# Random V blocks of 18 pairs: gathered by GpSimd with row lists, in place of SP's block transfers

## The chip, the cores and the metric

The kernel runs on one core of a Trainium2 chip. The metric is the device time of one execution in microseconds, taken as the median of the runs. Engines are called PE (TensorE), DVE (VectorE), ACT (ScalarE), POOL (GpSimd) and SP (SyncE).

## The reference

Block-sparse attention, and then a two-layer network over its output:

```python
batch, n_heads, seq, head_dim = (4, 8, 768, 64)
block, n_rand = 32, 3
n_blocks = seq // block                                   # 24
rand_blocks = np.random.randint(0, n_blocks, size=(n_blocks, n_rand))

scores = scale * np.matmul(q, k.transpose(0, 1, 3, 2))
mask = np.abs(blk_i - blk_j) <= 1
mask = mask | (blk_i == 0) | (blk_j == 0) | (blk_i == n_blocks - 1) | (blk_j == n_blocks - 1)
for qb in range(n_blocks):
    for kb in sampled_blocks[qb]:
        mask[qb * block:(qb + 1) * block, kb * block:(kb + 1) * block] = True
scores = np.where(mask, scores, -1e9)
attn = softmax(scores)
x = (attn @ v), heads side by side                        # 3072 x 512
h = x @ w_in                                              # 3072 x 2048
g = h * (1.0 / (1.0 + np.exp(-beta * h)))
return (g @ w_out).astype(np.float32)                     # 3072 x 512
```

The three random key blocks of a query block are the same for all heads and all batches, and are known only at run time.

## The kernel before

**Pairs.** The 22 inner query blocks of a batch are handled two at a time: 11 pairs per batch, 44 pairs `n` in all, pair `n` being pair `p` of batch `b`. For each of its two query blocks (`g` = 0, 1) a pair needs eight key blocks: three random ones, three neighbours, and the first and the last block. Pairs 26 to 32 belong to the third batch, pairs 33 to 43 to the fourth.

**Steps of a pair.** POOL copies the random K blocks out of the transposed K (`kg`, L634); POOL or DVE copies the neighbours (`kn`, L312). PE computes the scores (`sc`, L753 for the mask, L763 for Q·K). DVE takes the maximum (`mx`, L776), ACT the exponential (`ex`, L784), DVE the reciprocal (`rc`, L801), POOL or DVE multiplies by it (`nrm`, L807). PE transposes the probabilities (`tp`, L821), DVE or ACT brings them to SBUF (`ptv`), PE multiplies with V (`av`, L848 from pair 16 on, 16 matmuls per pair), and DVE and ACT write the result into `xT`. There are three buffers for the K blocks and for the probabilities.

**V.** Each batch's V is stored to a table `VT[b]` in DRAM (L594), with the 512 numbers of all heads of one token in a row. The tile of a pair, `VG`, has four buffers from pair 8 on, so its transfers wait for `av` of pair `n - 4`. In it 96 partitions hold the three random blocks and 96 the three neighbours of each `g`; 32 more hold the first and the last block, which stay in place within a batch: three later pairs of a batch copy them on DVE (`vres`, L312 with `VG<-VG`). From pair 4 on the random blocks come by six transfers from SP, 32 rows of 1 KB each, whose addresses SP has loaded into registers for up to two pairs at a time (`vv`, L663). All transfers of `VG` are L714.

**The first and last query blocks** attend to all keys. They are handled per batch (L911 to L971); their matmuls with V (L965) wait for DVE's copies into `PTG` (L953).

**The network** runs in eight groups `G` of tokens (256 or 512 tokens): PE's h (L1027), ACT's tanh (L1033), DVE's product (L1038), PE's y (L1054). ACT scales each 128 x 512 result (`oe`, L316) and SP stores it (`od`, L1072; L1074 and L1075 where the rows are split into two stores). The last result of the run is of the split kind. Groups wait for the `xT` columns of their pairs.

**The order.** Every step is a task with an engine or a choice of engines, a duration, a priority and dependencies. `Plan.run` plays the tasks through with these durations and fixes the order of each engine's instructions and, where a task has a choice, its engine; on the chip every engine then works through its own list in order, and semaphores do the waiting. `Plan.OFFSET` shifts the priorities of single tasks.

Of the kernel before, what the change touches and what calls it, by code (L numbers as in the profile page):

```python
# [216 lines left out]
def kernel(  # L217
# [11 lines left out]
    nc = tc.nc  # L229
# [31 lines left out]
    NHOT, NV = 0, 2  # L261
    NHL, UP = 4, 1024.0
    WIDE = 16

# [33 lines left out]
    t_sb = [sb(f"t{i}", [P, 512]) for i in range(NT)]  # L298
    osb = [sb(f"osb{i}", [P, D_MODEL], FP32) for i in range(NO)]
    VT = [dram.tile([S, D_MODEL], FP16, name=f"VT{b}") for b in range(B)]  # L300
    banks = [psum.tile([P, 512], FP32, name=f"bank{i}") for i in range(8)]
# [88 lines left out]
    for part, f in enumerate((emit_mask0, emit_mask1, emit_mask2)):  # L390
# [135 lines left out]

    trK, trQ, evK, evQ, vperm, vtab = {}, {}, {}, {}, {}, {}
    later = {b: [] for b in range(B)}
    for b in range(B):
        pr = prep_prio(b)  # L530
        if b:
            vperm[b] = []
            for nm, t, raw in (("V", v, RV), ("K", k, RK), ("Q", q, RQ)):
                tr = {"K": trK, "Q": trQ}.get(nm)
                for f in range(2):
# [18 lines left out]
        for nm, s16, dstT, tr, ev in (("K", RK, KT, trK, evK), ("Q", RQ, QT, trQ, evQ)):  # L554
            for hp in range(NHP):
                def emit_tr(nm=nm, s16=s16, b=b, hp=hp):
# [22 lines left out]
        if b == 0:  # L579
            vperm[0], vtab[0] = [], []  # L580
            for f in range(2):
                cs = slice(f * HH * D, (f + 1) * HH * D)
                vperm[0].append(add(f"vperm0.{f}", "DVE", 0.95, lambda f=f, cs=cs: copy_on(
                    "DVE", Vn[0][:, :, cs].rearrange("p j (h d) -> p h j d", h=HH),
                    v_stage[:, f * HH:(f + 1) * HH, :].rearrange("p h (j d) -> p h j d", j=J)),
                    deps=[v0ld[f]], prio=-73))
                vtab[0].append(add(f"vtab0.{f}", "SP", 0.45, lambda cs=cs, vt_rows=vt_rows: nc.sync.dma_start(
                    out=vt_rows[:, :, cs], in_=Vn[0][:, :, cs]),
                    deps=[vperm[0][f]], prio=-77.5, dma=0.95, hw=1))

            for f in range(2):
                ld0["Q", f].deps += vperm[0][:QV[f]]
        else:
            vtab[b] = [add(f"vtab{b}", "SP", 0.4, lambda b=b, vt_rows=vt_rows: nc.sync.dma_start(  # L594
                out=vt_rows, in_=Vn[b % 2]), deps=vperm[b], prio=pr + 5, dma=1.9, slack=1.0, hw=1)]

# [12 lines left out]
    order_pairs = [(b, p) for b in range(B) for p in range(NPAIR)]  # L609
    xlate, picks = [], []  # L610
    held_n, vv, vv_of, vg_last = {}, None, None, None
    RND = 0.18
# [3 lines left out]
    for n, (b, p) in enumerate(order_pairs):  # L616
# [10 lines left out]

        def emit_kg(b=b, p=p, kt32=kt32, kg32=kg32):
            _, vals = nc.values_load_multi_w_load_instructions(
                offP[0:1, p, 0:6], engines=(ET.Pool,), min_val=0, max_val=(NB - 1) * W,  # L630
                skip_runtime_bounds_check_because="block numbers lie below the number of blocks")
            for g in range(2):
# [29 lines left out]
        def emit_vv(n=n, p=p):  # L662
# [3 lines left out]
                skip_runtime_bounds_check_because="block numbers lie below the number of blocks")[1]  # L666
        if n >= NSEL and (p % NV == 0 or n == NSEL):
            held_n[n] = min(NV - p % NV, NPAIR - p)
            vv = add(f"vv{n}", "SP", 0.7 + 0.03 * 6 * (held_n[n] - 1), emit_vv,
                     deps=[t_idx] + (vg[n - 4] if n >= 4 else []), prio=-45.5 if n < NSEL + 4 else pr - 1)  # L670
            vv_of = n
        elif n < NSEL:
            vv = None

        vt = VT[b]

        def moves(n=n, vgb=vgb, vt=vt, i0=i0, first=head_v, w0=6 * (n - vv_of) if n >= NSEL else 0):
            if first and n >= 2 * NVG:
# [18 lines left out]
            elif i0 + 1 < NB - 2:  # L697
                yield 0.6, lambda v: (
                    vgb[0:3 * BLK, :, 1, :],
                    bass.AP(tensor=vt.tensor, offset=vt.offset + (i0 - 1) * BLK * D_MODEL,  # L700
                            ap=[[D_MODEL, 3 * BLK], [BLK * D_MODEL, 2], [1, D_MODEL]]))
            else:
                yield 0.3, lambda v: (vgb[0:3 * BLK, 0, 1, :], vt[(i0 - 1) * BLK:(i0 + 2) * BLK, :])
                yield 0.1, lambda v: (vgb[0:BLK, 1, 1, :], vt[(NB - 1) * BLK:NB * BLK, :])
                yield 0.2, lambda v: (vgb[BLK:3 * BLK, 1, 1, :], vt[i0 * BLK:(i0 + 2) * BLK, :])
# [5 lines left out]
        for k_, (cost, f) in enumerate(moves()):  # L711
            def emit_vg(vv_of=vv_of if n >= NSEL else None, f=f):
                o, i = f(held.get(vv_of))
                nc.sync.dma_start(out=o, in_=i)  # L714
            vg[n].append(add(f"vg{n}.{k_}", "SP", 0.5, emit_vg,
                             deps=[vv] + vtab[b] + ([av[vlast(n)]] if vlast(n) >= 0 else []) +
                             ([ld["Q", 0, hp] for hp in range(NHP)] if NVG <= n < 2 * NVG else []),
                             prio=vprio(n, k_), dma=cost, hw=1))

# [95 lines left out]
        def emit_tp(n=n, pb=pb):  # L815
            o = bank16(("T", n))
            for g in range(2):
                for c in range(2):
                    for u in range(2):
# [3 lines left out]
        tp[n] = add(f"tp{n}", "PE", 0.45, emit_tp, deps=[nrm[n]] if nrm[n] else [ex[n, 0], ex[n, 1]], prio=pr - 0.5, lat=0.2,  # L823
                    opens=(("T", n),))
        ptv[n] = add(f"ptv{n}", {"DVE": 0.61, "ACT": PTA}, None, lambda eng, n=n: copy_on(
            eng, PT[n % NPT], bank16(("T", n))),
            deps=[tp[n]] + ([av[n - NPT]] if n >= NPT else []), prio=pr - 0.5, closes=(("T", n),))

        wide = n >= WIDE

        def emit_av(n=n, vgb=vgb, wide=wide, late=late, hl=HL[n % NHL]):
            o = bank(("O", n))
            pt = PT[n % NPT].rearrange("x (g c u m) -> x g c u m", g=2, c=2, u=2)

# [65 lines left out]
    for b in range(B):  # L900
        for w, (blk, u) in enumerate((bl, u) for bl in (NB - 1, 0) for u in range(2)):
# [28 lines left out]
            def emit_ge(m=m, s_=s_, pg=pg):  # L930
                for hf in range(2):
                    nc.scalar.activation(  # L932
                        out=pg[:, hf * (S // 2):(hf + 1) * (S // 2)], in_=bank(("GS", m, hf))[:, 0:S // 2],
                        func=AF.Exp, bias=s_[:, 2:3], scale=1.0, accum_out=s_[:, 3 + hf:4 + hf])
# [12 lines left out]
            def emit_gt(m=m, pg=pg):  # L947
                o = bank16(("GT", m))
                pj = pg[:, :].rearrange("x (p j) -> x j p", j=J)
                for j in range(J):  # L950
                    nc.tensor.transpose(out=o[:, j * P:(j + 1) * P], in_=pj[:, j, :], identity=identity)
            gt[m] = add(f"gt{m}", "PE", 0.34, emit_gt, deps=[gn[m]], prio=pr, lat=0.2, opens=(("GT", m),))
            gptv[m] = add(f"gptv{m}", "DVE", 0.47, lambda m=m, w=w: nc.vector.tensor_copy(  # L953
# [37 lines left out]
    for b in range(2, B):  # L991
        old = [x[n] for n, (bb, _) in enumerate(order_pairs) if bb == b - 2 for x in (kg, kn)] + gsc_all[b - 2]
        oldq = [sc[n] for n, (bb, _) in enumerate(order_pairs) if bb == b - 2] + gsc_all[b - 2]
        for hp in range(NHP):
            trK[b, hp].deps += old
            trQ[b, hp].deps += oldq
        for t in vperm[b]:
# [11 lines left out]
    for G, sz in enumerate(sizes):  # L1009
# [38 lines left out]
        for s in range(sz // 4):  # L1048
# [20 lines left out]

            def emit_od(ob=ob, base=base, row=row):  # L1070
                if row + P <= S:
                    nc.sync.dma_start(out=out[base + row:base + row + P, :], in_=ob)  # L1072
                else:
                    nc.sync.dma_start(out=out[base + row:base + S, :], in_=ob[0:S - row, :])  # L1074
                    nc.sync.dma_start(out=out[base:base + row + P - S, :], in_=ob[S - row:P, :])  # L1075
            out_dma.append(add(f"od{G}.{s}", "SP", 0.9 if row + P > S else 0.45, emit_od, deps=[te],
                               prio=at(0.5 + 2.0 * s / sz), slack=ODS, dma=0.7, hw=2 if row + P > S else 1))
            nout += 1
# [35 lines left out]
```

## Time and profile before

| | us |
|---|---|
| median of 3 runs | 307.89 (307.64 to 308.00) |
| the profiled execution | 306.66 |
| its span | 304.9 |
| PE busy | 284.7 (93%) |
| DVE busy | 241.3 (79%) |
| ACT busy | 219.8 (72%) |
| POOL busy | 172.9 (57%) |
| transfers of 32 KB into VG from SP, landing | 220, median 2.6 |

The profiled execution is one run with the profiler on; its time beside the span has 1.76 us at the start and the end that the span leaves out. An engine's busy time counts the instructions that compute; POOL's transfers count as busy while POOL prepares them, SP's do not. Matmuls overlap in the pipeline, so a busy PE is one that has work without a gap.

### The profile page before, as it was taken

To read this page: it belongs to the slowest core of one execution; us is meant where nothing else is said; L and a number is where in the kernel's file an instruction comes from. 1 tells how busy PE (TensorE), PEld (TensorE's weight loads), DVE (VectorE), ACT (ScalarE), POOL (GpSimd) and SP (SyncE) were. 2 spreads that over 40 slices of the span, in tenths; PEclk is the share of its full clock that TensorE was granted. 3 is DMA by queue.
4 is the path that set the end of the run, shared out by engine and by line. 5 is a ranking of instruction groups with operands and counts; after the bars stand their busy time and mean duration, and the time that the engine had idled before them with its cause. 6 is when DMAs were issued, how large, how long until landed. Compare 5 with 4: busy or idle time off the path is not lost.

```text
span 304.9 us, 11891 instructions
## 1 busy us (share of the span) xinstructions
PE 284.7 (93%) x4209; PEld 177.3 (58%) x4209; DVE 241.3 (79%) x562; ACT 219.8 (72%) x639; POOL 172.9 (57%) x513
## 2 busy tenths in 40 slices
PE   2699869999999899999998999999999999999994
PEld 0455658657855785665556555556555555554671
DVE  4857989999999999999999579989789765780260
ACT  3347669889788999898759599978689837771461
POOL 3079895044689678899784486868646942100000
PEclk9999979999999999999999999999999999999999
DMA  7999999978999462479943633234343242101202
GB/s 254 370 295 207 233 208 231 221 219 136 165 208 183 119 190 74 123 145 166 210 124 116 203 123 97 73 85 124 100 155 106 75 121 90 37 0 57 83 1 69
DMA packets 43445, 44.17 MB, mean 145 GB/s; under 512 B 6005, under 2 KB 39414, under 8 KB 43386
## 3 DMA queue, kind: packets, MB, share of 16 engines
q1 hardware_dynamic: 31056, 32.13, 35.1%
q0 software_dynamic: 12320, 11.27, 24.8%
q8 instruction: 33, 0.54, 0.7%
q14 instruction: 26, 0.21, 0.2%
q10 hardware_dynamic: 10, 0.01, 0.0%
HBM read 45.23 MB, written 9.44 MB: 179 GB/s over the span
## 4 chain that ended last, share of the span: by engine, by line
PE 70%; DVE 18%; DMA 6%; issue 2%; ACT 2%; SPq 1%; POOL 0%; DVEq 0%
PE bank L1027 26%; PE bank L1054 20%; PE bank L821 5%; DMA VG<-VT 4%; DVE ST L776 4%; PE bank L848 4%; PE bank L560 3%; PE bank L729 3%; DVE SG L925 3%; DVE VG L312 3%; DMA g<-in_k_dram 3%; PE bank L753 2%; PE bank L763 2%; PE bank L856 2%; DVE PTG L953 2%
## 5 line engine op out<-in xcount | busy, mean ns | idle before, releaser
L784 ACT ACTIVATE PP<-bank,ST 128x256 f16<-128x256 f32 x176 | 81.4, 479 | 20.6 <-DVE ST L776 12.4
L1027 PE MATMUL bank<-xT,w_in_sb 128*128 128x256 f16 (+1 forms) x512 | 94.0, 328 | 1.4 <-DVE g L1038 0.9
L1054 PE MATMUL bank<-w_out_sb,g 128*128 128x512 f16 x384 | 92.3, 380 | 0.0
L1038 DVE SCALAR_TENSOR_TENSOR g<-t,bank 128x512 f16<-128x512 f16 (+1 forms) x128 | 66.5, 546 | 19.4 <-ACT t L1033 19.0
L1033 ACT ACTIVATE t<-bank,beta_sb 128x512 f16<-128x512 f32 (+1 forms) x128 | 70.4, 594 | 13.5 <-PE bank L1027 9.6
L807 POOL TENSOR_SCALAR PP<-PP,ST 128x256 f16<-128x256 f16 x132 | 63.4, 497 | 27.6 <-DVE ST L801 27.6
L634 POOL COPY KG<-KT 128x64 f32 x264 | 52.0, 247 | 32.4 <-PE bank L763 18.8
L1027 PEld LDWEIGHTS <-w_in_sb 128*128 128x128 f16 x512 | 53.7, 115 | 25.8 <-issue 4.6
L776 DVE TENSOR_REDUCE ST<-bank 128x2 f32<-128x512 f32 x88 | 57.4, 680 | 3.4 <-PE bank L763 2.1
L1054 PEld LDWEIGHTS <-g 128*128 128x128 f16 x384 | 34.4, 98 | 38.2 <-issue 4.9
L784 ACT ACTIVATION_READ_ACCUMULATOR PP<-bank,ST 128x1 f32 x176 | 37.0, 210 | 0.0
L316 ACT ACTIVATE osb<-bank 128x512 f32<-128x512 f32 x24 | 14.5, 605 | 19.6 <-PE bank L1054 19.5
L312 DVE COPY PT<-bank 128x1024 f16<-128x1024 f16 x39 | 26.7, 685 | 2.4 <-PE bank L821 1.6
L821 PE MATMUL bank<-identity,PP 128*128 128x128 f16 x352 | 28.0, 224 | 0.3 <-ACT PP L784 0.3
L943 POOL TENSOR_SCALAR PG<-PG,SG 128x768 f16<-128x768 f16 x16 | 14.4, 900 | 23.9 <-ACT PG L932 19.8
L821 PEld LDWEIGHTS <-PP 128*128 128x128 f16 x352 | 22.8, 100 | 7.6 <-issue 1.3
L312 DVE CAST xT<-bank 64x256 f16<-64x256 f32 (+1 forms) x33 | 13.9, 420 | 8.4 <-ACT xT L310 7.4
L848 PEld LDWEIGHTS <-VG 128*128 128x128 f16 x448 | 16.5, 98 | 6.7 <-DMA VG<-VT 1.0
L932 ACT ACTIVATE PG<-bank,SG 128x384 f16<-128x384 f32 x32 | 18.3, 585 | 2.4 <-DVE SG L927 2.2
L312 POOL COPY KG<-KT 128x384 f32<-128x384 f32 (+3 forms) x47 | 19.6, 438 | 0.4 <-PE bank L763 0.4
L763 PE MATMUL bank<-KG,QT 64*32 64x256 f16 x704 | 18.0, 269 | 1.1 <-issue 1.1
L848 PE MATMUL bank<-PT,VG 128*128 128x64 f16 x448 | 17.7, 193 | 0.1
(107 smaller groups left out, 309.8 us busy)
## 6 DMA issues: line engine op xcount, KB each, us to landing
VG<-VT SPq DMA_DIRECT2D x220, 32.0 KB, 2.6
VG<-VT SPq DMA_DIRECT2D x32, 192.0 KB, 2.6
out_dram<-osb SPq DMA_DIRECT2D x20, 256.0 KB, 2.4
RV<-in_v_dram POOLq DMA_DIRECT2D x6, 384.0 KB, 6.4
RK<-in_k_dram POOLq DMA_DIRECT2D x6, 384.0 KB, 8.3
VT<-Vn SPq DMA_DIRECT2D x3, 768.0 KB, 3.9
RQ<-in_q_dram POOLq DMA_DIRECT2D x6, 384.0 KB, 6.4
w_in_sb<-in_moe_w_in_dram POOLq DMA_DIRECT2D x8, 256.0 KB, 8.0
```

The costliest lines, as they stand in the source:

```text
L312: (nc.vector if eng == "DVE" else nc.gpsimd).tensor_copy(out=out, in_=in_)
L634: nc.gpsimd.tensor_copy(out=kg32[:, g, :, (SR + r) * W:(SR + r + 1) * W], in_=kt32[:, :, bass.ds(vals[3 * g + r], W)])
L763: nc.tensor.matmul(bk[u][hp * BLK:(hp + 1) * BLK, g * 256:(g + 1) * 256], lhsT=QT[b % 2][u * D:(u + 1) * D, hp, (i0 + g) * BLK:(i0 + g + 1 ...
L776: mx[n, u] = add(f"mx{n}.{u}", "DVE", 0.6, lambda n=n, u=u, sb_=sb_: nc.vector.tensor_reduce(out=sb_[:, 0, 2 * u:2 * u + 2], in_=bank(("S" ...
L784: nc.scalar.activation(out=pb[:, u, g, :], in_=bank(("S", n, u))[:, g * 256:(g + 1) * 256], func=AF.Exp, bias=sb_[:, 0, 2 * u + g:2 * u + ...
L807: (nc.vector if eng == "DVE" else nc.gpsimd).tensor_scalar(out=pb[:, u, g, :], in0=pb[:, u, g, :], scalar1=sb_[:, 2, 2 * u + g:2 * u + g + ...
L821: nc.tensor.transpose(out=o[:, s * P:(s + 1) * P], in_=pb[:, u, g, c * P:(c + 1) * P], identity=identity)
L848: nc.tensor.matmul(o[:, (g * NHP + hp) * 2 * BLK:(g * NHP + hp + 1) * 2 * BLK], lhsT=vgb[:, g, c, hp * P:(hp + 1) * P], rhs=pt[:, g, c, :, ...
L1027: nc.tensor.matmul(o[:, 0:TW], lhsT=w_in_v[:, c, f // 4, f % 4, :], rhs=xT[:, c, c0:c0 + TW], start=(c == 0), stop=(c == NHP - 1))
L1033: lambda G=G, f=f, TW=TW, tt=tt: nc.scalar.activation(out=tt[:, 0:TW], in_=bank(("H", G, f))[:, 0:TW], func=AF.Tanh, bias=0.0, scale=beta_ ...
L1038: lambda G=G, f=f, TW=TW, tt=tt, gg=gg: nc.vector.scalar_tensor_tensor(out=gg[:, f, 0:TW], in0=tt[:, 0:TW], scalar=1.0, in1=bank(("H", G, ...
L1054: nc.tensor.matmul(o[:, :], lhsT=gg[:, f, s * P:(s + 1) * P], rhs=w_out_sb[:, f, :], start=(f == 0), stop=(f == N_FFC - 1))
```

## The change

From pair 26 on (`IG`), the random V blocks are fetched by POOL's indirect transfers. Each takes a list of 96 row numbers, one per partition, and fetches the 96 rows of `VT[b]`; there are two per pair, one for each `g`. The lists are columns of a tile `rows96`, made once near the start: POOL writes a few constants (`rowc`), PE adds 32 x block number and the row within the block by four matmuls of one row (`rows`), DVE copies them as integers (`rowlist`). SP's register loads end with pair 25. The plan books POOL with 0.9 us for each of these transfers; they wait for the list, the table and `av` of pair `n - 4`. The neighbours and the edge blocks stay with SP.

Three further edits are active. The eight transposes of a pair come in the order `u, g, c`, and the matmuls with V read accordingly. The exponential of the first and last query blocks is written in the order in which it is transposed, so that ACT reads PSUM with a stride and PE's transposes read contiguously. The last result of the run is scaled in halves by ACT and DVE, and its two stores are issued by SP and ACT. The plan's duration for the tables of V is 0.45 in place of 0.40.

The diff also brings paths that its constants turn off (`TD`, `GD`, `KD`, `NBP`, `ODP`, and `TBE = "SP"`): transposes by DMA and plain transfers from POOL. They are left out here. Its core:

```diff
+    IG, IGT = 26, 0.9
+    NI = NB - 2
+    rows96 = sb("rows96", [3 * BLK, NI], I32)
+    cE = sb("cE", [1, 4, 3 * BLK])
+    sf16 = sb("sf16", [1, 3, NI])
+    mi96 = sb("mi96", [1, 3, BLK], I32)
+
+    def emit_rc():
+        V = nc.gpsimd
+        V.iota(mi96, pattern=[[0, 3], [1, BLK]], base=0, channel_multiplier=0, allow_small_or_imprecise_dtypes=True)
+        V.memset(cE[:, 0:3, :], 0.0)
+        for r_ in range(3):
+            V.memset(cE[:, r_, r_ * BLK:(r_ + 1) * BLK], float(BLK))
+        V.tensor_copy(out=cE[:, 3, :], in_=mi96[:, :, :].rearrange("o r m -> o (r m)"))
+        V.tensor_copy(out=sf16, in_=sf[:, :, :].rearrange("o a r -> o r a"))
+    t_rc = add("rowc", "POOL", 1.0, emit_rc, deps=[t_idx], prio=60)
+
+    def emit_rows():
+        o_ = bank("rows")[0:3 * BLK, 0:NI]
+        for r_ in range(3):
+            nc.tensor.matmul(o_, lhsT=cE[0:1, r_, :], rhs=sf16[0:1, r_, :], start=(r_ == 0), stop=False)
+        nc.tensor.matmul(o_, lhsT=cE[0:1, 3, :], rhs=ones[0:1, 0:NI], start=False, stop=True)
+    t_rows = add("rows", "PE", 0.2, emit_rows, deps=[t_rc, t_ident], prio=80, lat=0.2, opens=("rows",))
+    t_list = add("rowlist", "DVE", 0.1, lambda: nc.vector.tensor_copy(
+        out=rows96, in_=bank("rows")[0:3 * BLK, 0:NI]), deps=[t_rows], prio=80, closes=("rows",))
...
-        if n >= NSEL and (p % NV == 0 or n == NSEL):
-            held_n[n] = min(NV - p % NV, NPAIR - p)
+        if NSEL <= n < max(IG, 2 * NVG) and (p % NV == 0 or n == NSEL):
+            held_n[n] = min(NV - p % NV, NPAIR - p, max(IG, 2 * NVG) - n)
...
-            for g in range(2 if n >= NSEL else 0):
+            for g in range(2 if n >= max(IG, 2 * NVG) else 0):
+                yield 0.5, (lambda v, g=g, p=p: (vgb[0:3 * BLK, g, 0, :], vt[:, :], rows96[:, 2 * p + g:2 * p + g + 1])), 3
+            for g in range(2 if NSEL <= n < max(IG, 2 * NVG) else 0):
                 for r in range(3):
...
+            eng = "POOL" if (n >= max(NBP, 2 * NVG) and where) or where == 3 else "SP"
...
+                if where == 3:
+                    o, i, rows_ = f(None)
+                    nc.gpsimd.indirect_dma_start(
+                        out=o, out_offset=None, in_=i, in_offset=bass.IndirectOffsetOnAxis(ap=rows_, axis=0))
+                    return
...
+            vg[n].append(add(f"vg{n}.{k_}", eng, 0.5 if eng == "SP" else IGT if where == 3 else 0.65, emit_vg,
+                             deps=([vv] if eng == "SP" and vv else [kg[n]] if where == 2 else [t_list] if where == 3 else []) + vtab[b] + ([av[vlast(n)]] if vlast(n) >= 0 else []) +
                              ([ld["Q", 0, hp] for hp in range(NHP)] if NVG <= n < 2 * NVG else []),
-                             prio=vprio(n, k_), dma=cost, hw=1))
+                             prio=vprio(n, k_), dma=cost, hw=int(eng == "SP")))
...
-                        s = (g * 2 + c) * 2 + u
+                        s = (u * 2 + g) * 2 + c
...
                     nc.scalar.activation(
-                        out=pg[:, hf * (S // 2):(hf + 1) * (S // 2)], in_=bank(("GS", m, hf))[:, 0:S // 2],
+                        out=pg[:, :].rearrange("x (j p) -> x j p", j=J)[:, :, hf * hw_:(hf + 1) * hw_],
+                        in_=bank(("GS", m, hf))[:, 0:S // 2].rearrange("x (p j) -> x j p", j=J),
                         func=AF.Exp, bias=s_[:, 2:3], scale=1.0, accum_out=s_[:, 3 + hf:4 + hf])
...
+            if G == len(sizes) - 1 and s == sz // 4 - 1 and row + P > S:
+                te.emit, te.on = lambda ob=ob, G=G, s=s: scale_on(
+                    "ACT", ob[:, 0:256], bank(("Y", G, s))[:, 0:256], 0.5), {"ACT": 0.35}
+                tf = add(f"of{G}.{s}", "DVE", 0.35, lambda ob=ob, G=G, s=s: scale_on(
+                    "DVE", ob[:, 256:512], bank(("Y", G, s))[:, 256:512], 0.5), deps=list(te.deps), prio=te.prio,
+                    closes=(("Y", G, s),))
+                for q, en, r0, r1, d0 in ((nc.sync, "SP", 0, S - row, base + row), (nc.scalar, "ACT", S - row, P, base)):
+                    out_dma.append(add(f"od{G}.{s}{en}", en, 0.45, lambda q=q, ob=ob, r0=r0, r1=r1, d0=d0: q.dma_start(
+                        out=out[d0:d0 + r1 - r0, :], in_=ob[r0:r1, :]), deps=[te, tf], prio=te.prio, dma=0.4, hw=1))
```

More of the change, by code (lines that the diff above doesn't have):

```diff
@@ L262 @@
     NHL, UP = 4, 1024.0
+    by_dma = lambda n: n >= TD[0] and n % TD[1] < TD[2]
+    TD = (99, 1, 1)
+    GD = 9
+    KD = 9
+    IG, IGT = 26, 0.9
+    TBE = "SP"
+    tq = lambda: nc.sync if TBE == "SP" else nc.gpsimd
+    tbk = dict(dma=1.9, hw=1) if TBE == "SP" else dict(dma=1.9)
+    NBP, ODP, RP = 99, (), 0
     WIDE = 16
@@ L299 @@
     osb = [sb(f"osb{i}", [P, D_MODEL], FP32) for i in range(NO)]
+    KQ = [dram.tile([NHP, S, P], FP16, name=f"KQ{i}") for i in range(2)]
     VT = [dram.tile([S, D_MODEL], FP16, name=f"VT{b}") for b in range(B)]
@@ L610 @@
     xlate, picks = [], []
+    held_k = {}
     held_n, vv, vv_of, vg_last = {}, None, None, None
```

125 lines of the change are left out of this document (91 added, 34 removed).

## The prediction

> **What bounds the kernel now.** I read the page first, then the windows view by stage, then the waits of TensorE (PE), the timelines of GpSimd (POOL) and SyncE (SP), and the end of the run.
>
> ```profile
> span 304.9 us, 11891 instructions
> PE 284.7 (93%) x4209; PEld 177.3 (58%) x4209; DVE 241.3 (79%) x562; ACT 219.8 (72%) x639; POOL 172.9 (57%) x513
> ...
> PE   2699869999999899999998999999999999999994
> ...
> POOL 3079895044689678899784486868646942100000
> ```
>
> PE's row is 9 almost throughout from the twelfth slice; POOL's row has room in the second half. The windows (columns: start:end, length, then busy time and count of PE, PEld, DVE, ACT, POOL) say where:
>
> ```profile
> 120.00:150.00 30.00, 29.81 (x427) 17.15 (x425) 29.41 (x69) 26.35 (x84) 27.41 (x75) 1.00 0.78 154
> 150.00:165.00 15.00, 14.18 (x242) 8.73 (x242) 14.47 (x32) 9.64 (x32) 9.86 (x27) 1.00 0.52 124
> ...
> 210.00:225.00 15.00, 14.51 (x223) 9.02 (x222) 12.41 (x25) 10.12 (x29) 9.90 (x28) 1.00 0.40 117
> ...
> 155.00:247.00 92.00, 90.69 (x1320) 53.26 (x1319) 78.08 (x158) 70.97 (x214) 63.02 (x192) 1.00 0.39 115
> ```
>
> From 150 to the last matmul at 300.9 PE stands still for 0.82 + 0.49 = 1.3 us, and the waits view of that stretch names the whole of it:
>
> ```profile
> PE bank L965 <- DVE PTG L953: 1.3, 3, 0.8
> ```
>
> No matmul there waits for V: the transfers that the change touches are hidden already. The rest of PE's idle time (some 15 us) lies before 150, and 4.0 us behind the last matmul.
>
> The change acts from the gathers of pair 26, which wait for the P·V matmuls of pair 22. L848 has 16 matmuls per pair, from pair 16 on; the windows by that line have 22 pairs left at 150, so pair 22 is the first of them, at 154.3. The last gather, for pair 43, waits for pair 39, at 246.2. So all of it falls in 155 to 247, the last row above.
>
> **Part by part: SP.** Taken off: 18 pairs x 6 = 108 transfers of 32 KB and ten register loads.
>
> ```profile
> 178.37 28.08 SPq L714 DMA_DIRECT2D VG<-VT  x45
> ...
> L663 SPq TENSOR_LOAD <-offV x22: 722/752/1995, 18.7 to 233.3; - x22
> ```
>
> 45 issues in 28.08 us are 0.62 us each; 108 x 0.62 + 10 x 0.75 = 75 us of SP's queue. On the path it is worth 0: pair n's blocks are asked for once pair n-4 is done, some 20 us (four pairs at 92/18 = 5.1 us) ahead, and they land 1.9 us after issue. What comes earlier is the output stores behind them, for which PE does not wait in this stretch (view above). If that cover were gone the landing time, 1.9 us, would show per pair.
>
> **POOL.** Added: 36 gathers of 96 rows. No view has one; the nearest rows are the plain transfers that POOL issues:
>
> ```profile
> L543 POOL DMA_DIRECT2D RQ<-in_q_dram x6 | 4.7, 789 | 0.0
> ...
> L519 POOL DMA_DIRECT2D w_out_sb<-in_moe_w_out_dram x8 | 4.1, 522 | 0.4 <-POOL w_out_sb L499 0.3
> ```
>
> Lower end 0.52 (64 partitions). Upper end 0.79 plus 0.75, the register load from memory above, as the price of reading the list: 1.54. I take 0.8: a gather has 96 pieces, fewer than RQ's 128 x 4, and reads a list on top. (The plan in the changed code books 0.9, which is no measurement.) Then 36 x 0.8 = 28.8, and POOL has 63.0 + 28.8 = 91.8 us of work in 92 us. It cannot be that full; the plan can give the copies of neighbouring K blocks to VectorE (DVE): those that POOL runs there sum to 9.0 us in its timeline. POOL and DVE together then hold 63.0 + 78.1 + 28.8 = 169.9 of 184 us, 92%. The row 120 to 150 held 27.41 + 29.41 = 56.8 of 60, 95%, with six transfers of POOL among them, and PE lost 0.19 us in 30. So I cost it at 0 on the path. The cover is gone where the two fill more than that row: 0.947 x 184 = 174.3, less 141.1, over 36 gives 0.92 us per gather. Above that PE, whose order is fixed, waits 36 us for each us of excess.
>
> A gather holds back what POOL has behind it, the K copies of the next pair (score matmuls wait for these) and the normalisation (1.84 us; the transposes wait for it), if its own waits come late: pair n-4, the table of V and the list. POOL stands still for 92 - 63 = 29 us there, mostly for DVE's reciprocals, so a gather of 0.8 fits such gaps in part. Its transfer meets no bulk load: in 155 to 247 no load of POOL is issued. Landing: 6.4 us is the median of RQ and RV, 1.9 that of the blocks now; both under 20.
>
> At one place POOL is slowed by DVE. First DVE's timeline, then POOL's, with start and duration in front:
>
> ```profile
> 155.66 0.93 DVE L312 COPY VG<-VG 32x2048 f16<-32x2048 f16 x1
> ```
>
> ```profile
> 154.69 2.69 POOL L807 TENSOR_SCALAR PP<-PP,ST 128x256 f16<-128x256 f16 x4
> ...
> 167.35 1.84 POOL L807 TENSOR_SCALAR PP<-PP,ST 128x256 f16<-128x256 f16 x4 [1.70 <-DVE ST L801]
> ```
>
> Four normalisations take 1.84 as a rule and 2.69 beside that copy: 0.85 lost of 0.93. Three such copies (pairs 34 to 36, after 209) fall among the gathers: at most 3 x 0.93 = 2.8 us more, 0.08 per gather, so 0.88, still under 0.92 but near. The Trainium skill, "SBUF — State Buffer", section "SBUF: two separate sides", says that a DMA issued from GpSimd cannot have its descriptors written while DVE holds the port pair that they share, and that SP's are immune; section "A bandwidth-pool intuition that's wrong" has one growing from about 620 to 3100 ns. By that, an estimate from the page, three gathers cost 2.5 us more each, a gather 1.0 on average and the sum 3 us more. The trace agrees for POOL's arithmetic (0.85 of 0.93 above) and shows no gather.
>
> The lists themselves: seven small operations on POOL at 0.13 to 0.24 each, about 1.4 us, behind `idx` at 3.5; POOL then stands idle for 11.7 us to 15.28. Four one-row matmuls (0.3 each by the start-to-start of L430) fall before PE's first transpose at 10.39, and one 0.2 us copy on DVE, which is idle for 0.8 before 9.77. Cost 0; 0.2 if the copy lands between the first casts.
>
> **The other edits.** The order of the pair's eight transposes and the strided read of the global rows' exponentials keep the counts. L316's evictions read PSUM strided already, 768 elements in 0.81 us against 512 contiguous ones in 0.60, no dearer per element: 0. Last output: now
>
> ```profile
> 300.89 0.60 ACT L316 ACTIVATE osb<-bank 128x512 f32<-128x512 f32 x1 [2.86 <-PE bank L1054]
> 301.51 0.33 SPq L1074 DMA_DIRECT2D out_dram<-osb  x1
> 301.89 0.42 SPq L1075 DMA_DIRECT2D out_dram<-osb  x1
> ```
>
> Halves on ScalarE (ACT) and DVE: 0.39 each (L316's 128x256 form has a median of 0.393) instead of 0.60, 0.2 saved. Both stores at once: the second, which lands 2.0 after 301.89, no longer comes last, but the first (2.3 after 301.51) does: 0.1 more. Sum 0.3; ends 0.2 and 0.6 (were both issue steps gained).
>
> **Sum.** The edits move the plan's order in the pairs, and the 1.3 us of PE's waits for PTG are redrawn; between 0 and all of it I take half, 0.6. On the profiled execution: 306.66 (span 304.9 and 1.76 around it) - 0.3 - 0.6 = 305.8. The median of the runs is 1.23 above that execution, so 307.0.
>
> **Rivals.** *POOL becomes the bound.* For it: 0.88 against 0.92, and 63 us of other work. Against: fewer pieces than any plain transfer's. Decides from 0.92 us per gather; at 1.03, 36 x 0.11 = 4.0, less 0.3: 311.6; at 1.1, 6.5 - 0.3: 314.1. Chance 0.15. *Gathers stretched by DVE's copies*, a place of its own: if all six copies of V's edge rows after 154 meet a gather, 6 x 0.93 / 36 = 0.16, so 0.96 each and 36 x 0.04 = 1.4, less 0.3: 309.0. The stretched normalisation speaks for it, that three of the six lie at the very start against it. Chance 0.06. (The page of the Trainium skill named above is the rule behind this one.) *The work given to DVE delays the pairs* (maximum, reciprocal and copies of transposes are on DVE, 96% busy in 150 to 165): 18 pairs with 0.1 us of wait each, 1.8 - 0.3: 309.4. Chance 0.12. *Only the end is saved*, since PE was full: 307.6, chance 0.12. That SP's queue bounded something unseen is against the waits view; it adds to the low end alone.
>
> **How the numbers follow.** The forecast has 0.55; about 0.6 us (0.2%) is what a measurement of this kernel can tell from none, and with more than 0.3 of the 1.3 regained it shows: 0.46 faster, 0.09 same. The last rival gives 0.11 same and 0.01 faster, the other three 0.33 slower. Faster 0.47, same 0.20, slower 0.33. The forecast's own range is 306.0 (0.6 and 1.3 regained) to 307.7 (0.2 and none). The whole reaches from 305.6 (0.4 more before 150, where PE has idle time and the plan books the tables of V at 0.45 and not 0.40, which may move the order) to 311.5, a gather of about 1.03.
>
> **What would show it.** Right: gathers of 0.7 to 0.9 us on POOL, PE idle below 1.3 us from 150 to its last matmul, neighbour K copies moved to DVE, SP's VG issues down by 108, the last store at about 301.3. Wrong: gathers over 0.92 us, POOL at 95% from 155 to 247, and PE's transposes waiting for POOL's PP; or PE waiting for DVE's ST in that stretch.

## The result and the profile after

The changed kernel took 325.35 us as the median (324.11 to 325.81), the kernel before 307.76 beside it: a ratio of 1.0577 (95% interval 1.0528 to 1.0625), 17.6 us slower, where 307.0 was predicted and 311.5 was the upper end. Three later comparisons of the same changed kernel gave 1.0255, 1.0213 and 1.0542; the two sizes are a finding of their own, taken up below.

The page after, the lines that answer to the first fence of the prediction:

```profile
span 324.0 us, 11614 instructions
PE 293.5 (91%) x4213; PEld 181.4 (56%) x4213; DVE 250.7 (77%) x578; ACT 218.6 (67%) x637; POOL 205.8 (64%) x544
...
PE   2699889999998999999989899698879989999994
...
POOL 4158992045788769999698598799978896200000
```

POOL has 32.9 us more of work, PE's row has 6, 7 and 8 in the second half where it had 8 and 9. The windows (columns as before) put it in the predicted stretch:

```profile
120.00:150.00 30.00, 29.87 (x437) 17.36 (x436) 29.44 (x73) 26.47 (x86) 27.89 (x81) 1.00 0.68 134
150.00:165.00 15.00, 14.16 (x192) 8.00 (x190) 14.60 (x30) 9.77 (x32) 11.78 (x24) 1.00 0.68 145
210.00:225.00 15.00, 13.84 (x193) 7.32 (x191) 14.45 (x33) 9.15 (x34) 13.75 (x33) 1.00 0.25 77
155.00:247.00 92.00, 81.70 (x1131) 46.35 (x1130) 72.97 (x148) 59.38 (x178) 77.46 (x174) 1.00 0.35 105
```

PE loses 10.3 us in 155 to 247 (before: 1.3), and with fewer matmuls done there it ends later. SP's part came as counted: 164 issues of `VG` from SP (272 before) and 12 register loads (22 before), the last at 152.0:

```profile
L802 SPq DMA_DIRECT2D VG<-VT x164: 304/316/1293, 15.9 to 265.8; - x164
...
L736 SPq TENSOR_LOAD <-offV x12: 725/752/1966, 18.8 to 152.0; - x12
```

The gather had no row before. First its group on the page, then three of them in POOL's timeline:

```profile
L798 POOL DMA_INDIRECT VG<-VT,rows x36 | 34.7, 965 | 8.2 <-issue 5.3
```

```profile
177.24 0.94 POOL L798 DMA_INDIRECT VG<-VT,rows  x1 [0.30 <-PE bank L943]
178.48 0.92 POOL L798 DMA_INDIRECT VG<-VT,rows  x1 [0.30 <-issue]
179.71 0.92 POOL L798 DMA_INDIRECT VG<-VT,rows  x1 [0.30 <-issue]
```

The reader should add two columns here. A gather is busy for 0.965 us on average, and POOL stands still for 8.2 us just before the 36: 0.16 ahead of a gather that follows arithmetic, 0.30 ahead of one that follows a gather (the releasers named there are long done, or "issue"). POOL is held for (34.7 + 8.2) / 36 = 1.19 us per gather; from one start to the next it is 1.23. The waits of PE from 155 on, where the old kernel had one line of 1.3 us, begin:

```profile
PE bank L1162 <- DVE xT L327: 2.8, 1, 2.8
PE bank L943 <- DVE PT L327: 1.7, 2, 0.9
PE bank L943 <- DVE ST L889: 1.2, 1, 1.2
PE bank L909 <- POOL PP L895: 1.1, 4, 0.5
PE bank L943 <- issue: 1.0, 1, 1.0
```

Few name POOL. The longest ends at a DVE cast (`xT`), and that cast stood behind copies of DVE that ran beside POOL's work. DVE's timeline, then POOL's:

```profile
203.54 2.88 DVE L327 COPY KG<-KT 128x256 f16<-128x256 f16 x3
206.46 0.43 DVE L327 CAST xT<-bank 64x256 f16<-64x256 f32 x1
```

```profile
203.56 1.12 POOL L707 COPY KG<-KT 128x64 f32 x6
204.67 2.01 POOL L895 TENSOR_SCALAR PP<-PP,ST 128x256 f16<-128x256 f16 x4
```

POOL goes without a gap from the gather at 202.62 to 206.7, and three neighbour copies of DVE take 2.88 us beside it; PE's y waits for the cast that follows them. In experiment 5 the same three took 1.35 us and POOL's copies 1.31 in place of 1.12. So the two seem to hold each other up, and which of them is held changes from run to run. Late landing is not the price: one weight load of PE waits for `VG` from 155 on (1.2 us, at 238.0), in experiment 11 none does.

### The profile page after: what moved, and what is told of

Same layout as the page of the kernel before. It is cut to its first block, busy times and chain, and to the rows that moved or that the text cites. A ratio compares the mean times of both kernels' runs of the same rounds, so it can differ in the third digit from the quotient of the medians.

```text
span 324.0 us, 11614 instructions
## 1 busy us (share of the span) xinstructions
PE 293.5 (91%) x4213; PEld 181.4 (56%) x4213; DVE 250.7 (77%) x578; ACT 218.6 (67%) x637; POOL 205.8 (64%) x544
## 4 chain that ended last, share of the span: by engine, by line
PE 51%; DVE 20%; DMA 8%; issue 7%; POOL 6%; ACT 5%; POOLq 2%; SPq 1%; DVEq 0%; ACTq 0%
PE bank L1162 17%; PE bank L1135 15%; PE bank L817 4%; DVE g L1146 4%; DMA VG<-VT 4%; PE bank L909 4%; DVE ST L864 3%; DVE SG L1020 3%; PE bank L943 3%; PE bank L629 3%; POOL KG L707 3%; DMA g<-in_k_dram 2%; DVE PT L327 2%; ACT PP L872 2%; DMA w_out_sb<-in_moe_w_out_dram 2%
## 5 line engine op out<-in xcount | busy, mean ns | idle before, releaser
L1135 PE MATMUL bank<-xT,w_in_sb 128*128 128x256 f16 (+1 forms) x512 | 95.4, 332 | 1.8 <-DVE g L1146 1.0
L707 POOL COPY KG<-KT 128x64 f32 x264 | 51.9, 245 | 20.4 <-DVE KT L327 10.6
L864 DVE TENSOR_REDUCE ST<-bank 128x2 f32<-128x512 f32 x88 | 57.6, 680 | 7.7 <-PE bank L1162 2.9
L1162 PEld LDWEIGHTS <-g 128*128 128x128 f16 x384 | 34.7, 98 | 41.6 <-issue 7.7
L798 POOL DMA_INDIRECT VG<-VT,rows x36 | 34.7, 965 | 8.2 <-issue 5.3
L327 DVE COPY PT<-bank 128x1024 f16<-128x1024 f16 x40 | 27.4, 684 | 6.7 <-PE bank L909 4.8
L909 PE MATMUL bank<-identity,PP 128*128 128x128 f16 x352 | 29.9, 228 | 2.1 <-POOL PP L895 1.1
L331 ACT ACTIVATE osb<-bank 128x512 f32<-128x512 f32 (+1 forms) x24 | 14.3, 596 | 21.9 <-PE bank L1162 21.0
L851 PE MATMUL bank<-KG,QT 64*32 64x256 f16 x704 | 19.4, 279 | 2.3 <-POOL KG L707 1.2
```

Source lines behind the costliest of these rows:

```text
L327: (nc.vector if eng == "DVE" else nc.gpsimd).tensor_copy(out=out, in_=in_)
L798: nc.gpsimd.indirect_dma_start(out=o, out_offset=None, in_=i, in_offset=bass.IndirectOffsetOnAxis(ap=rows_, axis=0))
L864: mx[n, u] = add(f"mx{n}.{u}", "DVE", 0.6, lambda n=n, u=u, sb_=sb_: nc.vector.tensor_reduce(out=sb_[:, 0, 2 * u:2 * u + 2], in_=bank(("S" ...
L909: nc.tensor.transpose(out=o[:, s * P:(s + 1) * P], in_=pb[:, u, g, c * P:(c + 1) * P], identity=identity)
L1135: nc.tensor.matmul(o[:, 0:TW], lhsT=w_in_v[:, c, f // 4, f % 4, :], rhs=xT[:, c, c0:c0 + TW], start=(c == 0), stop=(c == NHP - 1))
L1162: nc.tensor.matmul(o[:, :], lhsT=gg[:, f, s * P:(s + 1) * P], rhs=w_out_sb[:, f, :], start=(f == 0), stop=(f == N_FFC - 1))
```

## Experiments

Each comparison has its own runs of the kernel before (medians 307.4 to 308.0 us). The first four experiments shared a chip (A), the next eight another (B), the four after them chip A again, the last two a third (C); the chip of the first comparison was not recorded.

**1. All edits but the gathers.** `-    IG, IGT = 26, 0.9`, `+    IG, IGT = 99, 0.9`: no pair is gathered; the lists, the order of the transposes, the strided read, the split end stay.

> The changed kernel with IG = 99: the random V blocks of all pairs come from SP as before, the other edits stay (row lists, order of the transposes, strided exponential, split end, 0.45 booked for the tables). Theory A (a gather holds POOL for 1.23 us, 0.94 and a gap of 0.30, where the plan books 0.90): 307.4, 0.3 below the kernel before for the split end. Theory B (the redrawn order itself is poor, whatever a gather takes): 307.4 as well. Theory C (the 3 us that the changed kernel is behind at 150, before its first gather, come from the other edits): 310 to 311.

308.23 against 307.95 us, 1.0012 (0.9988 to 1.0037). The other edits neither cost nor gain what can be measured; the loss belongs to the gathers and what the plan makes of them.

**2. The gathers booked at 1.25 us.** `+    IG, IGT = 26, 1.25`: the plan knows about the true price.

> The changed kernel with 1.25 us booked for a gather in place of 0.90. Theory A: PE's order then fits what POOL does, so of the 17.6 us some 5 to 10 come back: 315 to 320. Theory B: another order, no rule for its sign: 320 to 330. Theory C: 325.

317.67 us, 1.0317 (1.0281 to 1.0354). A plan with the right duration does not find room for the work, though it loses less than the plan that books 0.9: the changed kernel took 325.3 us on the same chip (experiment 15).

**3. and 4. The changed order with a plain transfer, and with none.** In the changed order each gather is a plain POOL transfer of 96 fixed rows (experiment 3), or is left out (4); the blocks that `VG` holds are then not the selected ones.

```diff
-                    nc.gpsimd.indirect_dma_start(
-                        out=o, out_offset=None, in_=i, in_offset=bass.IndirectOffsetOnAxis(ap=rows_, axis=0))
+                    nc.gpsimd.dma_start(out=o, in_=i[0:3 * BLK, :])     # 3; in 4 nothing
```

> The changed kernel with its order unchanged; each gather is replaced by a plain transfer from POOL of the same 96 x 1 KB into the same place, from the first 96 rows of the table, so the random blocks of V from pair 26 on are not the drawn ones. Theory A: 0.5 to 0.6 us and a gap of 0.3 or less, at or under the 0.90 booked: 308 to 311. Theory B: as the changed kernel, 322 to 326. Theory C: 3 us over the kernel before, 311, if A holds otherwise.

> The changed kernel with its order unchanged; the gathers are left out, so from pair 26 on the random blocks of V are what the buffer held. Theory A: POOL is early everywhere, 307 to 309. Theory B: 322 to 326. Theory C: 310 to 311.

309.70 us, 1.0071 (1.0040 to 1.0102), and 310.48 us, 1.0072 (1.0047 to 1.0097). The plain transfer's group:

```profile
L798 POOL DMA_DIRECT2D VG<-VT x36 | 19.6, 547 | 2.1 <-PE bank L942 2.1
```

So the redrawn order by itself costs some 2 us. Without gathers PE waits 2.2 us from 155 on, all of it for DVE (1.3 before). Another 0.55 us of POOL per fetch is free. PE's waits show 0.9 of the 2 us; where the rest lies was not looked for. All that the changed kernel loses beyond this comes with the gather.

**5. The changed kernel again.** No edit.

> The changed kernel itself, beside the others on one chip, for its clock in the slices from 30 to 60 us (0.72 in its profile, 0.94 in the kernel before). If the lower clock belongs to the program: 324 to 326 and 0.7 again. If it was that chip's or that run's: about 322 and 0.9, and the 3 us by which its gathers began late are gone; the loss behind 150 stays 14 to 16 either way.

315.14 against 307.36 us, 1.0255 (1.0223 to 1.0287): the gathers are as long as before (965 ns), the loss is 10 us smaller. No reading of the expectation had that.

**6. A third of the rows.** `+ (vgb[0:BLK, g, 0, :], vt[:, :], rows96[0:BLK, 2 * p + g:2 * p + g + 1])`: each gather fetches 32 rows, two of three random blocks are left out.

> The changed kernel, order unchanged, with each gather cut to 32 of its 96 rows; the other 64 rows of the random blocks of V keep what the buffer held. If a gather's time on POOL is mostly a fixed part (reading the list, starting): 0.8 to 0.95 us and 320 or more. If it goes with the rows: 0.4 to 0.6 us and 308 to 312, as with plain transfers.

312.88 us, 1.0192 (1.0159 to 1.0226). The groups of POOL:

```profile
L798 POOL DMA_INDIRECT VG<-VT,rows x36 | 32.6, 905 | 8.3 <-issue 5.0 <-PE bank L1135 1.4 <-PE bank L943 0.9
```

64 rows fewer save 0.06 us of 0.965: the time is nearly all fixed, and shorter lists buy little, 5.5 us lost in place of 7.8. The duration came as expected for a fixed price, the total of 320 did not.

**7. Gathers from pair 35 on only.** `+    IG, IGT = 35, 1.25`: 18 gathers, where POOL has more room.

> The changed kernel with gathers from pair 35 only, 18 in place of 36, and 1.25 us booked. If the loss that stays with 1.25 booked from pair 26 on (9.7 us) is POOL's capacity, half the gathers in the half where POOL has more room cost little: 308 to 311. If each gather costs the same wherever it stands: 9.7 / 2 = 4.9, so 312.8. Other orders can add about 2 of either sign.

308.20 us, 1.0039 (1.0017 to 1.0060). Half the gathers cost 0.84 us, not half of the loss of experiment 5. Place and booking changed along with the number, but the reading is that of experiment 10 too: a gather has no price of its own on the path; what counts is whether POOL is full.

**8. SP freed and nothing added.** The kernel before, with its 108 random transfers from pair 26 on left out (those rows of `VG` are old).

```diff
+                if n >= 26 and cost == RND:
+                    return
```

> The kernel before, order unchanged, with SP's 108 transfers of random V blocks from pair 26 on left out (these blocks are what the buffer held). If SP's queue is off the path, as predicted: 307.9. If it held something back: 306 or less, and this would be the most that any change of who issues them can bring.

307.82 us, 1.0017 (0.9996 to 1.0039). In this order even a fetch that costs no engine anything would have gained nothing that can be measured.

**9. Two plain transfers per gather.** 48 fixed rows each, not the selected ones.

```diff
+                    nc.gpsimd.dma_start(out=o[0:48, :], in_=i[0:48, :])
+                    nc.gpsimd.dma_start(out=o[48:96, :], in_=i[48:96, :])
```

> The changed kernel in its order, each gather replaced by two plain GpSimd transfers of 48 fixed rows each (the same bytes into VG, not the selected blocks): 72 plain transfers in place of 36 gathers. One plain transfer of 96 rows took 0.547 us; if two of half the rows take 0.5 to 0.55 each, GpSimd is held 1.0 to 1.1 us per gather, as much as by the gather with its gap (0.94 to 0.97 and 0.16 to 0.30). Theory A (GpSimd's time counts, whatever takes it): as the changed kernel on the same chip within 2 us, 2 to 3% above before. Theory B (something of the gather itself costs, its gaps or its hold on DVE's copies): near the plain transfer's 1.007, at most 1.012.

311.13 against 307.65 us, 1.0125 (1.0095 to 1.0156): between the two theories. The pair holds POOL for 0.526 + 0.508 = 1.03 us, and no gap lies before either (groups of POOL):

```profile
L798 POOL DMA_DIRECT2D VG<-VT x36 | 18.9, 526 | 0.0
L799 POOL DMA_DIRECT2D VG<-VT x36 | 18.3, 508 | 0.0
```

**10. One gather per pair.** `+ if where == 3 and k_ % 2 == par: return`: the gather of `g` = 1 is left out.

> The changed kernel in its order, with the gather of g=1 of each pair left out (those rows of VG keep old values): 18 gathers. Theory A (GpSimd has room for about 0.8 us per gather, so for nearly one gather of 0.95 plus its gap per pair): 1.007 to 1.011, like the order without any gathers. If every gather costs a share of its own, whatever room there is: half way between 1.007 and the changed kernel of the same chip (about 1.016 or more).

309.71 us, 1.0055 (1.0035 to 1.0075): no dearer than the order without any gather (1.0072 on chip A).

**11. The changed kernel a third time.** No edit.

> The changed kernel unchanged, a third time. It gave 1.0577 in the first comparison and 1.0255 in the second. If the spread is a matter of the chip and of when PE's clock falls early: between the two, with every gather at 0.92 to 0.98 us again, and windows of 155 to 247 us with GpSimd at 13 to 14 of 15 us busy. If the first comparison was out of the ordinary: 1.02 to 1.03.

314.42 us, 1.0213 (1.0188 to 1.0238).

**12. The split end alone.** The kernel before with the last output's edit and nothing else.

> The kernel before with the last output alone split (half of its copy on DVE, half on ACT, its two stores on two queues); nothing else of the change. The prediction's term: 0.2 to 0.6 us less, ratio 0.998 to 0.9993. The rival reading after the run without gathers (1.0012): nothing measurable, within 0.2% of 1.

307.44 us, 0.9997 (0.9979 to 1.0015). The timeline at the end of this run:

```profile
300.39 0.38 ACT L316 ACTIVATE osb<-bank 128x256 f32<-128x256 f32 x1 [2.86 <-PE bank L1054]
300.80 0.42 DVE L318 TENSOR_SCALAR osb<-bank 128x256 f32<-128x256 f32 x1 [5.53 <-ACT osb L316]
301.25 0.33 SPq L1078 DMA_DIRECT2D out_dram<-osb  x1
301.26 0.38 ACTq L1078 DMA_DIRECT2D out_dram<-osb  x1
```

DVE begins its half when ACT's has ended: from the start of the scaling to the first store it is 0.86 us, against 0.62 with one piece. DVE waits for ACT's `osb`, so the halves are not side by side, and what the second store gains is spent. The plan set no such order between them; what put the wait there was not looked into.

**13. and 14. The gather's hold without a gather, and more than it.** Experiment 9 with a memset that nobody reads, and with three plain transfers of 32 rows.

```diff
+                    nc.gpsimd.memset(mi96[:, :, :].bitcast(FP16), 0.0)     # 13, behind the two of 9
+                    for r_ in range(3):                                    # 14, in their place
+                        nc.gpsimd.dma_start(out=o[r_ * BLK:(r_ + 1) * BLK, :], in_=i[r_ * BLK:(r_ + 1) * BLK, :])
```

> The changed kernel in its order, each gather replaced by two plain GpSimd transfers of 48 fixed rows (0.99 us together where they follow each other) and one memset of 192 elements that nobody reads (estimated 0.2 to 0.25 us from the 288 elements in 0.328 and the 128 in 0.195), so that GpSimd is held 1.19 to 1.24 us, as by the gather with its gap (1.23 start to start where two follow). The blocks fetched aren't the selected ones. Theory A (the hold alone): as the changed kernel of the same chip within 0.4%, 1.019 to 1.026. Theory B (a gather costs more than its hold): near the two plain transfers' 1.0125, at most 1.016.

> The changed kernel in its order, each gather replaced by three plain GpSimd transfers of 32 fixed rows, about 1.48 us of GpSimd per gather (0.50 for one where they follow). Not the selected blocks. Theory A, with GpSimd the bound beyond about 0.9 us per gather: 36 gathers longer by 0.49 us than two plain transfers make 17.6 us, most of it on the path: 1.04 to 1.07. If GpSimd's hold is mostly covered: 1.02 to 1.03.

316.83 against 307.78 us, 1.0282 (1.0218 to 1.0346); the memset took 0.264, so POOL was held 1.30 us per gather, 0.11 more than by the gather. The changed kernel took 325.3 on this chip (experiment 15), so here the hold alone, theory A, does not make the whole loss. Three transfers are (55.2 + 1.9 of gaps) / 36 = 1.59 us: 326.73, 1.0614 (1.0536 to 1.0691). The window of 13 shows POOL full:

```profile
155.00:247.00 92.00, 87.25 (x1216) 49.79 (x1214) 78.90 (x160) 66.43 (x198) 91.72 (x254) 1.00 0.35 107
```

With the plain transfers alone (experiments 4, 3, 9, 13, 14; only 9 ran on chip B) the loss against the time that POOL is held is: 2.5 us at 0, 1.8 at 0.55, 3.5 at 1.03, 9.1 at 1.30, 19.0 at 1.59: flat, then 0.57 us of loss per us held (over 36 fetches), then 1.0. Read off at the gather's 1.19 it gives 3.5 + 0.57 x 36 x 0.16 = 6.8 us. Experiment 11 lost 6.8, experiment 5 7.8; at the 1.136 of experiment 6 it gives 5.6, and 5.5 was measured. On chip B the hold explains the loss to within 1 us: a gather costs what any other work of that length on POOL costs.

**15. and 16. The changed kernel a fourth time, and the booking of 1.25 again**, on the chip of experiments 1 to 4.

> The changed kernel unchanged, a fourth time, for its spread and as the yardstick of this chip. 1.02 to 1.03 with no place where all engines stand still at once, or 1.05 to 1.06 with such places (0.44 and 0.90 us in the first profile, and the later order of the engines out of step).

> The gathers booked at 1.25 us, a second time. It gave 1.0317, with one standstill of all engines of 0.33 us after four gathers in a row. If booking the true price helps: at or below the changed kernel of this chip. If the standstill made its loss: 1.02 without it. If the longer booked order is itself worse: 1.03 again.

325.32 us, 1.0542 (1.0481 to 1.0604), as in the first comparison; 318.21 us, 1.0327 (1.0268 to 1.0387). Experiment 16 is 7 us below 15, as its first reading asked, but it has standstills as well, so it does not tell the three readings apart. In the slices between 30 and 60 us PE's clock was 0.94 in this run (0.72 in the first), so the early clock is not the cause of the 10 us. From 155 to 247 it was 0.96 here and 1.00 in the first, with the same loss. The timelines of PE, DVE and POOL in experiment 15:

```profile
178.91 0.28 PE L851 MATMUL bank<-KG,QT 64*32 64x256 f16 x5
180.01 0.45 PE L851 MATMUL bank<-KG,QT 64*32 64x256 f16 x11 [0.82 <-issue]
```

```profile
176.70 0.43 DVE L327 CAST xT<-bank 64x256 f16<-64x256 f32 x1 [2.34 <-ACT xT L325]
180.10 1.29 DVE L864 TENSOR_REDUCE ST<-bank 128x2 f32<-128x512 f32 x2 [2.97 <-PE bank L1162]
```

```profile
178.06 0.92 POOL L798 DMA_INDIRECT VG<-VT,rows  x1 [0.30 <-issue]
178.99 0.58 POOL L707 COPY KG<-KT 128x64 f32 x3
180.23 0.59 POOL L707 COPY KG<-KT 128x64 f32 x3 [0.66 <-PE bank L1162]
```

PE stops after five of sixteen matmuls of one group, POOL after three of six copies, DVE before a maximum whose scores PE had ended at 176.2; all three go on within 0.25 us. From 179.57 to 180.01, and again for 0.89 us from 237.86, no engine computes. The first profile has the same two places (0.44 and 0.90 us), each at the end of four gathers in a row. Experiments 2 and 16 have two each as well (0.33 and 0.23; 0.21 and 0.39), the first behind four gathers in a row, the second behind two. The profiles of experiments 5 and 11 have none, with the same rows of gathers. In DVE's timeline of experiment 11 that maximum starts at once:

```profile
176.86 1.29 DVE L864 TENSOR_REDUCE ST<-bank 128x2 f32<-128x512 f32 x2
```

The standstill itself is short, but DVE had been idle for 2.97 us by then, and ACT, which waits for that maximum, stood 4.21. Experiments 15 and 11 run the same instructions, so that the starts of the same instructions can be compared along the run, here those of six of DVE's maxima:

| start of a maximum (DVE, L864), us | 1 | 2 | 3 | 4 | 5 | 6 |
|---|---|---|---|---|---|---|
| experiment 11 | 160.50 | 176.86 | 195.42 | 205.51 | 222.19 | 230.71 |
| experiment 15 | 160.10 | 180.10 | 198.26 | 210.81 | 227.05 | 238.92 |
| 15 behind 11 | -0.40 | 3.24 | 2.84 | 5.30 | 4.86 | 8.21 |

At the end it is 10.2 (spans 324.2 and 314.0), 10.6 us in all. 3.6 of them come between columns 1 and 2, at the first place, and 3.4 between 5 and 6, at the second; 2.5 come between 198 and 211, where there is no standstill of all engines. Experiment 5 stays 0.65 to 0.68 us ahead of 11 at all six. PE alone stops more often: from 155 on, its waits end at "issue", so at no releaser that the profile shows, five times in experiment 15 (3.4 us together) and four times in the first profile (2.2), beside pairs of gathers and once beside a single one too. In experiments 5, 11 and 17 no wait of PE there ends so.

**17. and 18. Rows of gathers broken up; SP's neighbours left out.** In 17 every second gather is experiment 13's substitute, so no two follow each other and there are 18; in 18 all gathers stay, and the neighbour blocks of V of pairs 26 on are not fetched.

```diff
+                    if k_ % 2 == 0:      # 17
+                        nc.gpsimd.dma_start(out=o[0:48, :], in_=i[0:48, :])
+                        nc.gpsimd.dma_start(out=o[48:96, :], in_=i[48:96, :])
+                        nc.gpsimd.memset(mi96[:, :, :].bitcast(FP16), 0.0)
+                        return
...
+                if n >= max(IG, 2 * NVG) and eng == "SP":      # 18
+                    return
```

> The changed kernel in its order with every second gather (g=1) replaced by two plain transfers of 48 fixed rows and a memset of 192 elements (1.3 us in the padded run), so that no two gathers follow each other and GpSimd's hold stays about that of the changed kernel. Half of the blocks aren't the selected ones. If rows of gathers cause the standstills and this runs on the chip that showed them: 1.022 to 1.032 and no place where all engines stand still. If single gathers cause them, or the hold alone does: such places again and 1.04 to 1.06. On the chip that never showed them: 1.02 to 1.03 either way, which tells nothing.

> The changed kernel in its order with SP's transfers of the neighbour blocks of V left out for the pairs from 26 on (VG keeps old rows there); all 36 gathers stay. If SP's transfers beside the gathers cause the standstills, on the chip that showed them: none, and 1.02 to 1.035. If the gathers alone cause them: two again, near 180 and 238 us, and 1.045 to 1.06. On the other chip 1.02 to 1.026 either way.

17: 315.73 against 307.77 us, 1.0265 (1.0230 to 1.0300), and no standstill. Its hold, the mean of 1.20 and 1.32 us, gives 8.2 us by the line above; 8.0 was measured. 18, on the same chip: 322.26 us, 1.0493 (1.0435 to 1.0550), with standstills at both places (0.31 and 0.61 us). The timelines of PE, DVE and POOL at the first:

```profile
178.51 0.51 PE L853 MATMUL bank<-KG,QT 64*32 64x256 f16 x4
179.47 0.44 PE L853 MATMUL bank<-KG,QT 64*32 64x256 f16 x12 [0.45 <-issue]
179.55 1.29 DVE L866 TENSOR_REDUCE ST<-bank 128x2 f32<-128x512 f32 x2 [2.83 <-PE bank L1164]
179.68 0.59 POOL L707 COPY KG<-KT 128x64 f32 x3 [0.54 <-PE bank L1164]
```

On the chips that show them the standstills come with gathers that follow each other. They don't need SP's neighbour transfers, and the hold doesn't make them (13 has more hold and none). That it is the row, and not that 17 has half as many gathers, was not tried apart. What it is that all engines wait for is open: no record names it, nor why one of three chips does not show it. That they come from a wait of the program is unlikely, since the same program runs through without them on that chip.

## Why the prediction was wrong

**The step that failed is POOL's term**: "I take 0.8: a gather has 96 pieces, fewer than RQ's 128 x 4", and from it "So I cost it at 0 on the path". The price was 1.19 us (0.965 busy, 0.23 standing), inside the bounds of 0.52 and 1.54 and above the point of 0.92 that the prediction itself had named for the change of sign. The reason given for 0.8 took a price per piece, which experiment 6 refutes: 0.06 us for 64 rows. And it looked for busy time alone; the 0.16 to 0.30 us before each gather is a fifth of the hold. The Trainium skill, "DMA: Bandwidth & Descriptors", section "Anatomy of one DMA — SWDGE (gpsimd) path", calls the share of descriptor generation in a transfer small and variable, with the write receipt as most of about 2 us; for the time to landing (2.5 to 5.1 us in experiment 11) that may do, but what decided here was the 1.19 us on POOL.

**The rival "POOL becomes the bound" was the right one**, with 0.15. At 1.1 us it gave 314.1, and the repeats on chip B measured 314.4 and 315.1. That the figures meet is partly luck: the price was 1.19, and by its rule of 36 us for each us beyond 0.92 that would have cost 9.7. Experiments 9 and 13 show the passage to be softer, 0.57 us per us, before it becomes 1.0. Its signs came too: POOL 91.72 of 92 us busy in experiment 13, and 84.20 with 7.0 us of gaps before the gathers in experiment 11, where PE's transposes waited 1.0 us for PP. Experiments 7 and 10 fit it from the other side: half the gathers cost no more than the order does. One reading beside it was off: POOL's 29 us of standing were not mostly for DVE's reciprocals (14.0), nearly as much was for PE's scores (13.4).

**What no step had** is what comes with the standstills, 8 to 11 us on two of three chips: 17.5 us lost in experiment 15 and 14.5 in 18, of which the hold explains 6.8. Some 7 us of it come at the two places themselves in experiment 15; what makes them is open. Without them the result would still have lain above the range, as on chip B.

**"Gathers stretched by DVE's copies" fell as a cause.** The median gather is 0.94, and one of 36 took 1.29; the length is in all of them. That one did meet a copy of the edge rows (DVE's timeline after the change, then POOL's):

```profile
160.90 0.88 DVE L327 COPY VG<-VG 32x2048 f16<-32x2048 f16 x1
```

```profile
161.41 1.29 POOL L798 DMA_INDIRECT VG<-VT,rows  x1 [0.17 <-issue]
```

The copy had 0.37 us to go when the gather began, and the gather took 0.35 longer than the median: 0.01 us per gather over the 36, where the rival had 0.16, and far from the estimate of 2.5 us for each of three. DVE was stretched beside POOL as well (2.88 us above). The rule of the Trainium skill behind that rival ("SBUF — State Buffer", section "SBUF: two separate sides"), that whichever starts first holds the shared port pair and the other blocks, fits the gather; for the three copies the order of starts was not worked out. It does not explain the standstills: section "Who interferes with whom" of the same page of the Trainium skill has a `tensor_reduce` on trn2 never contend, and the instruction that DVE could not start for 2.97 us was one.

**The order's term had the wrong sign.** The sum took 0.6 us off for PE's waits for PTG; experiments 3 and 4 show 1.8 to 2.5 us on. That is the size of the rival "work given to DVE delays the pairs" (1.8 us); DVE got the neighbour copies (41 instead of 29), and the waits of PE that were left are for DVE. That these copies alone are the cause was not tried.

**The end**: "Halves on ScalarE (ACT) and DVE: 0.39 each" were taken side by side, and they run one after the other (experiment 12); 0.3 us was forecast, and nothing that can be measured came (0.9979 to 1.0015). **Right** were SP's queue at 0 (experiment 8: 1.0017), the lists at 0 (POOL has them done at 4.7 us, DVE's copy takes 0.17 at 13.65; experiment 1: 1.0012), and the other edits at 0.

## What to carry to other kernels

Before moving transfers off an engine that nobody waits for, leave them out, as in experiment 8, and see what there is to gain: here it was nothing. Price an operation by start to start, idle time just before it included, and where the price is unknown near the point that decides, give the far side a chance to match. Work added to POOL went from free (75.6 of 92 us busy, experiment 3) to one for one (91.72 of 92, experiment 13) within some 0.75 us per operation. Since rows are nearly free, fewer and larger indirect transfers should be better, and other work between them may spare the standstills; neither was tried with all the rows fetched.

## What the runs showed of the hardware

- An indirect gather issued by POOL is busy 0.905 us with 32 rows of 1 KB and 0.965 with 96, behind a gap of 0.16 us (after arithmetic) or 0.30 (after a gather). A plain transfer of 48 rows takes 0.51 to 0.53 us on average and follows without a gap. One gather that began while DVE still had 0.37 us of a copy from SBUF to SBUF to do took 1.29.
- On two of three chips DVE was idle for 2.8 to 4.3 us and ACT for 4.1 to 5.0 beside four gathers in a row (the first of the two places, experiments 2, 15, 16 and 18), and all engines stood still for 0.2 to 0.4 us; a place of 0.2 to 0.4 us behind two gathers is in experiments 2 and 16. On the third chip the same rows ran through. The cause is open. Gathers with other POOL work between them (experiment 17) showed no such place.
- Three copies of DVE from SBUF to SBUF took 2.88 us in one run and 1.35 in another, beside the same instructions of POOL, whose six copies took 1.12 us in the first and 1.31 in the second.
